# The first token tile in two halves on two DMA queues, the second tile behind it on ScalarE's queue

## Chip, cores and metric

The kernel runs on one core of one Trainium2 chip. The metric is the device time of one execution in microseconds (us); lower is better. All times here come from the profile, from the trace behind it, or from timed runs of the kernel.

## What is computed

A transformer block with attention and a gated feed-forward layer side by side, over 2048 tokens of width 576, in bfloat16:

```python
xn  = layernorm(x)                       # eps 1e-5, no weights
qkv = xn @ wqkv                          # 32 heads of 18, q, k and v
p   = softmax(mask(q @ k.T * 18**-0.5))  # causal, window of 256 tokens
A   = (p @ v) @ wo
B   = (silu(xn @ w1) * (xn @ w3)) @ w2   # inner width 4608
out = x + A + B
```

## The kernel before

The tokens go in four chunks of 512, each of four tiles of 128 tokens (one token per partition). For each chunk the kernel normalises the four tiles, transposes them so that the width lies on partitions (`xnT`, and `xnS`, the same with the halves of the partitions swapped), projects q, k and v, runs the 36 units of the feed-forward layer's first stage (line L712) with the score, exponent and value steps of attention spread among them, and then the second stage with `w2` and `wo` (L778). The normalisation and transposes of chunks 1 to 3 are done during the chunk before; only those of chunk 0 stand in front of everything. Most matmuls work on 64 rows, two at a time on the two halves of the array.

The program is written as a list of operations. `add` appends one to its engine ("sp", "act", "pe", "dve", "pool": SyncE, ScalarE, TensorE, VectorE, GpSimd) together with the buffers it reads (`r`), writes first (`w`) or writes jointly with others (`j`). From these the waits are worked out; each engine runs its operations strictly in the order of the list. DMAs are issued on SyncE's or ScalarE's queue, and each buffer `xp0` to `xp6` has a semaphore of its own for its DMAs: a reader waits for the count that all its writers add up to. A DMA that an engine issues is one of its instructions, and what stands behind it on that engine comes after the issue.

The start of chunk 0, in the order of the list as far as the change touches it:

- GpSimd makes the identity (L280, L281) for the transposes and the constant -0.5 for the power.
- `load_x` (L292) fetches tiles 0 to 3 of `x`, 128 rows of 1152 bytes each: tile 0 on SyncE's queue, tiles 1, 2 and 3 on ScalarE's. SyncE goes on with the value weights `wv` (L821, L825), the query and key weights (L847, L851, into the buffer `pt`) and later the feed-forward weights (L316).
- VectorE clears `oq` (L827) and the query buffer `qv` (L828). TensorE runs nine matmuls on the zeros of `oq` (`warm`, L832) whose results nobody reads, then two more that wait for tile 0's variance.
- Tile 0's statistics are taken on VectorE (`ln_stats`: two halves with L376, their sum with L379, plus epsilon in L356). Tile 1's are taken on ScalarE (`ln_stats_act`): one pass for the mean (L366), one for the variance (L368), each with an accumulator read, and a small GpSimd operation (L370) that turns the first sum into the mean. Tiles 2 and 3 are done on VectorE.
- `ln_root` raises variance plus epsilon to the power -0.5 on GpSimd (L358).
- `ln_apply` writes the normalised tile `xn` (L399 on VectorE: 512 columns, then the last 64 twice). For tile 1 the last 64 columns go another way: GpSimd computes a shift (L391) and ScalarE applies it (L394).
- `xn_turn` transposes a tile with ten small matmuls (L414); the last pair takes the last 64 columns. ScalarE copies the result to `xnT` in two parts (L427); for tile 3 VectorE copies one of them.
- `warm_halves` (L838) is two more matmuls on zeros. `proj_begin` and `proj_end` run the two parts of a projection (L476); the four tiles' value projections alternate with the transposes, and q and k follow.

The order in the list around the change is written out by hand: tile 0's statistics, the two waiting matmuls, tile 1's statistics on ScalarE, the power of tile 0, the application of tile 0, the power of tile 1, the transposes of tile 0, the first part of its value projection, then VectorE's first half of tile 2's statistics, the application of tile 1, and so on. Nothing but this order and the waits sets when an instruction runs.

Of the kernel before, what the change touches and what calls it, by code (L numbers as in the profile page):

```python
# [44 lines left out]
class _Prog:  # L45
# [13 lines left out]
    def add(self, eng, fn, r=(), w=(), j=(), dma=None, after=()):  # L59
        deps = []  # L60
        for k in r:
            deps += self.bufs[k].writers
        for k in w:
            g = self.bufs.get(k)
            if g is not None:
                deps += g.ahead(eng)
        for k in j:
            g = self.bufs[k].before
            if g is not None:
                deps += g.ahead(eng)  # L70
        op = _Op(eng, fn, deps + list(after), dma)
        op.after = tuple(after)
        self.n[eng] += 1
        op.pos = self.n[eng]
        if dma is not None:
            self.dma_count[dma] = self.dma_count.get(dma, 0) + 16
            op.cnt = self.dma_count[dma]
        for k in r:
            self.bufs[k].readers.append(op)
        for k in w:  # L80
            self.bufs[k] = _Gen([op], self.bufs.get(k))
        for k in j:
            self.bufs[k].writers.append(op)
        for k in w:
            if self.bufs[k].before is not None:
                self.bufs[k].before.before = None
        self.ops.append(op)
        return op
# [76 lines left out]
def bass_parallel_sum__sliding_block__glu_gated_swiglu__prompt_kernel(  # L165
# [27 lines left out]
    x2 = A_x[0]  # L193
    out2 = out[0]
    P = _Prog(nc)
    add = P.add

    with ExitStack() as es:

        def sb(name, shape, dtype=dt.bfloat16):  # L200
            return es.enter_context(nc.sbuf_tensor(name, shape, dtype))
# [4 lines left out]
        xp = [sb(f"xp{i}", [128, D]) for i in range(NXP)]  # L206
# [78 lines left out]

        xp_ctr = 0

        def load_x(t, eng="sp"):
            nonlocal xp_ctr
            s = xp_ctr % NXP  # L290
            xp_ctr += 1
            add(eng, lambda e: e.dma_start(xp[s][:], x2[t * 128:(t + 1) * 128, :]), w=[("xp", s)], dma=f"xp{s}")  # L292
            return s

        nfill = 0
# [57 lines left out]
        def ln_root(t, eng=None):  # L353
            i = t % 2
            if eng is not None:
                return add(eng, lambda e: e.tensor_scalar(vpe[i][:], mv[i][:, 1:2], 1e-5, None, op0=ALU.add),  # L356
                           r=[("mv", i)], w=[("vpe", i)])
            return add("pool", lambda e: e.tensor_tensor(rstd[i][:], vpe[i][:], neghalf[:], ALU.pow),  # L358
                       r=[("vpe", i), "neghalf"], w=[("rstd", i)])

        def ln_stats_act(t, s):
            i = t % 2
            junk = hT[:, 0:3, :].rearrange("p t c -> p (t c)").bitcast(dt.float32)[:, 0:D]
            keys = [("h", n) for n in range(3)]
            root = float(D) ** 0.5
            add("act", lambda e: e.activation(junk, xp[s][:], ACT.Copy, scale=-1.0 / (D * root), accum_out=vpe[i][:]),  # L366
                r=[("xp", s)], w=[("vpe", i), *keys])
            add("act", lambda e: e.activation(junk, xp[s][:], ACT.Square, bias=vpe[i][:], scale=1.0 / root, accum_out=mv[i][:, 1:2]),  # L368
                r=[("xp", s), ("vpe", i)], w=[("mv", i), *keys])
            add("pool", lambda e: e.tensor_scalar(mv[i][:, 0:1], vpe[i][:], -root, None, op0=ALU.mult),  # L370
                r=[("vpe", i)], j=[("mv", i)])

        def ln_stats(t, s, part):
            i = t % 2
            if part < 2:
                add("dve", lambda e: e.bn_stats(stats[i][:, part, :], xp[s][:, part * HD:part * HD + HD]),  # L376
                    r=[("xp", s)], **{"j" if part else "w": [("stats", i)]})
                return
            add("dve", lambda e: e.bn_aggr(mv[i][:], stats[i][:]), r=[("stats", i)], w=[("mv", i)])  # L379
            if t >= TB:  # L380
                ln_root(t, "pool")
                ln_root(t)

        def ln_apply(t, s, parts=(0, 1)):

            i = t % 2
            for n in parts:
                both = xn[i][:, 512:640].rearrange("p (a c) -> p a c", a=2)
                end = xp[s][:, 512:D].unsqueeze(1).to_broadcast([128, 2, 64])
                if n == 2:  # L390
                    add("pool", lambda e: e.tensor_scalar(  # L391
                        shift[i][:], mv[i][:, 0:1], rstd[i][:, 0:1], -1.0, op0=ALU.mult, op1=ALU.mult),
                        r=[("mv", i), ("rstd", i)], w=[("shift", i)])
                    add("act", lambda e, dst=both, src=end: e.activation(  # L394
                        dst, src, ACT.Identity, bias=shift[i][:], scale=rstd[i][:, 0:1]),
                        r=[("xp", s), ("shift", i), ("rstd", i)], w=[("xnd", i)])
                    continue
                dst, src = (both, end) if n else (xn[i][:, 0:512], xp[s][:, 0:512])
                add("dve", lambda e, dst=dst, src=src: e.tensor_scalar(  # L399
                    dst, src, mv[i][:, 0:1], rstd[i][:, 0:1], op0=ALU.subtract, op1=ALU.mult),  # L400
                    r=[("xp", s), ("mv", i), ("rstd", i)], w=[("xnd" if n else "xn", i)])
# [415 lines left out]

        xslot = {}
        for t in range(TB):
            xslot[t] = load_x(t, "act" if t else "sp")  # L820
        add("sp", lambda e: e.dma_start(  # L821
            wv[:, 0:4, :], A_wqkv[0:512, 2 * D:3 * D].rearrange("(kd p) f -> p kd f", p=128)),
            w=["wv"], dma="wv")
# [6 lines left out]
        def warm(b, n, after=()):  # L830
            for k in range(n):
                add("pe", lambda e: e.matmul(PS[:, b, :], oq[:, 0:128], oq[:], start=True, stop=True),  # L832
                    r=["oq0"], after=after, **{"j" if k else "w": [("ps", b)]})
# [10 lines left out]
        for h in range(2):  # L844
            for n in range(2):
# [3 lines left out]
                    dma=f"wqk{h}", **{"j" if n else "w": [f"wqk{h}"]})  # L849
# [34 lines left out]
        for p in range(3):  # L884
            ln_stats(0, xslot[0], p)
        warm(4, 2, (ln_root(0, "dve"),))
        ln_stats_act(1, xslot[1])
        ln_root(0)
        ln_apply(0, xslot[0])
        ln_root(1, "pool")  # L890
        ln_root(1)
# [67 lines left out]
        for c in range(NC):  # L959
# [70 lines left out]
            for u in range(NF):  # L1030
# [3 lines left out]
                if u in loads:  # L1034
                    for i in loads[u]:
                        xslot[(c + 1) * TB + i] = load_x((c + 1) * TB + i)
# [12 lines left out]
                if next_pv in pv_ready and clock >= pv_ready[next_pv] and next_pv < 3:  # L1049
                    j = next_pv  # L1050
# [20 lines left out]
                if u in stat:  # L1071
                    t = (c + 1) * TB + stat[u]
# [4 lines left out]
                if u in apply:  # L1077
                    t = (c + 1) * TB + apply[u]
# [5 lines left out]
                if c == 0 and u == 13:  # L1084
                    for t in range(4):
# [3 lines left out]
                            dma="wo", **{"j" if t else "w": ["wo"]})  # L1089
                if c == 0 and u == 18:  # L1090
                    rows = A_wo[0:4 * Dh, :].rearrange("(n d) f -> n d f", d=Dh)
                    add("sp", lambda e: e.dma_start(wo[126:128, 0:4, :], rows[:, 0:2, :].rearrange("n d f -> d n f")),
                        j=["wo"], dma="wo")
                    for p in range(2):
                        add("sp", lambda e, p=p: e.dma_start(wo[64 * p:64 * p + 64, 4, :], rows[:, 2:Dh, :]),
                            j=["wo"], dma="wo")
                if c == 0 and u in (20, 22, 24, 26):
                    load_w2(0, (u - 20) // 2, "act" if u < 24 else "sp")
                if u == 31:
                    xs = [load_x(c * TB + tt) for tt in range(TB)]  # L1100
# [9 lines left out]
            n = -3  # L1110
            for item in p2_list(c):
# [25 lines left out]
                elif n in (100, 120) and c + 2 < NC:  # L1137
                    t = (c + 2) * TB + (n == 120)
# [34 lines left out]
```

## Time and profile before

| What | Value |
|---|---|
| Median of 3 runs | 558.82 us (558.53 to 558.98) |
| The profiled execution's own time | 558.68 us |
| Its span in the profile | 556.9 us |
| TensorE busy | 552.9 us, 99% of the span |
| VectorE, ScalarE, GpSimd busy | 310.2, 255.1, 163.5 us |
| DMA | 86.07 MB, mean 155 GB/s |
| First matmul of the projections (L476) | starts at 6.96 us |
| First matmul of the feed-forward stage (L712) | starts at 21.41 us |

Busy time is the time in which an engine has an instruction of its own under way. Matmuls are pipelined, so a busy TensorE also holds the time in which one waits for its turn in the array; how far it is from its best is read from the distance between starts. In the timeline a row is a group of like instructions: its start, its time, engine, line, operation, tiles written and read, shape and count, and in brackets the idle time before it and what ended it. "SPq" and "ACTq" are the issues of DMAs on the two queues; the time of an issue is that of the issuing engine and not of the transfer. "PEld" are weight loads of TensorE.

### The profile page before, as it was taken

Reading aid. Unit: us, or ns where it says so; the run is one execution under the profiler, and the core shown is the slowest. Engines: PE = TensorE matmul, PEld = TensorE weight load, DVE = VectorE, ACT = ScalarE, POOL = GpSimd, SP = SyncE. Lnnn points to the kernel's source line nnn. Section 1 sums busy time; section 2 is a strip of 40 time slices with the busy share of each in tenths; the row PEclk is TensorE's granted clock in tenths of the full one; section 3 lists DMA queues with packets and bytes.
Section 4 is the critical chain, followed back from the end, with each engine's and each line's share of the span. In section 5 each row is a group of like instructions: output and inputs, shape, how many; then the busy total and the mean of one; then the engine's idle time right before and its main releaser. Section 6 shows DMA issues by size and latency. Waiting matters only on the chain.

```text
span 556.9 us, 18212 instructions
## 1 busy us (share of the span) xinstructions
PE 552.9 (99%) x8013; PEld 351.1 (63%) x8013; DVE 310.2 (56%) x584; ACT 255.1 (46%) x357; POOL 163.5 (29%) x384
## 2 busy tenths in 40 slices
PE   8999999999999999999999999999999999999998
PEld 4566445677687455477777645547777654555776
DVE  7566788710466778851056668884105567767211
ACT  5357776100287776600047776650005667676000
POOL 6413454400033445330003344533000333433000
PEclk9999999999999999999999999999999999999999
DMA  9997999578566656656846746467683674551650
GB/s 247 210 189 167 206 206 217 144 180 190 137 136 144 145 137 160 156 147 178 201 109 140 171 110 170 124 162 160 171 195 86 137 171 124 151 135 31 164 151 22
DMA packets 127893, 86.07 MB, mean 155 GB/s; under 512 B 35430, under 2 KB 125502, under 8 KB 127814
## 3 DMA queue, kind: packets, MB, share of 16 engines
q1 hardware_dynamic: 88994, 62.88, 48.8%
q10 hardware_dynamic: 38820, 22.02, 16.1%
q8 instruction: 63, 1.03, 0.8%
q14 instruction: 16, 0.13, 0.1%
HBM read 71.37 MB, written 2.36 MB: 132 GB/s over the span
## 4 chain that ended last, share of the span: by engine, by line
PE 99%; DVE 0%; ACT 0%; issue 0%
PE ps L712 51%; PE ps L778 29%; PE ps L476 10%; PE ps L596 6%; PE ps L653 4%; PE ps L832 1%; PE ps L414 0%; DVE ofin L797 0%; ACT xnT L427 0%; DVE oq L827 0%
## 5 line engine op out<-in xcount | busy, mean ns | idle before, releaser
L712 PE MATMUL ps<-xnT,w 64*128 64x512 bf16 x1400 | 182.7, 376 | 0.0
L712 PE MATMUL ps<-xnS,w 64*128 64x512 bf16 x1120 | 155.6, 376 | 0.0
L778 PE MATMUL ps<-w,hT 64*128 64x288 bf16 x2288 | 143.7, 283 | 0.0
L727 DVE SCALAR_TENSOR_TENSOR gs<-th,ps 128x512 bf16<-128x512 bf16 x144 | 98.0, 681 | 80.2 <-ACT th L721 78.8
L605 ACT ACTIVATE pt<-ps 128x1024 bf16<-128x1024 f32 (+1 forms) x112 | 113.3, 1011 | 63.7 <-PE ps L596 62.7
L778 PEld LDWEIGHTS ps<-w,hT 64*128 64x128 bf16 x2288 | 111.9, 94 | 29.4 <-issue 0.2
L712 PEld LDWEIGHTS ps<-xnT,w 64*128 64x128 bf16 x1400 | 75.0, 94 | 53.9
L632 POOL TENSOR_TENSOR pt<-pt,mk 128x128 int32<-128x128 int32 (+1 forms) x199 | 80.6, 427 | 79.3 <-ACT pt L605 79.3
L730 DVE SCALAR_TENSOR_TENSOR hT<-gs,ps 128x512 bf16<-128x512 bf16 x144 | 98.9, 687 | 4.9
L721 ACT ACTIVATE th<-ps 128x512 bf16<-128x512 f32 x144 | 85.5, 593 | 23.5 <-PE ps L712 23.2
L712 PEld LDWEIGHTS ps<-xnS,w 64*128 64x128 bf16 x1120 | 61.0, 94 | 49.3
L797 DVE TENSOR_TENSOR ofin<-ps,xp 128x288 bf16<-128x288 f32 x32 | 12.7, 452 | 125.7 <-PE ps L778 125.7
L489 ACT ACTIVATE stage<-ps 128x512 bf16<-128x512 f32 x16 | 9.6, 598 | 143.6 <-PE ps L476 143.6
L632 POOL TENSOR_TENSOR hT<-hT,mk 128x128 int32<-128x128 int32 (+1 forms) x31 | 12.4, 422 | 169.7 <-ACT hT L605 169.7
L596 PE MATMUL ps<-qv,kv 64*128 64x320 bf16 (+4 forms) x528 | 54.0, 260 | 0.0
L596 PEld LDWEIGHTS ps<-qv,kv 64*128 64x128 bf16 x528 | 28.9, 94 | 24.1 <-ACT pt L605 0.3
L476 PE MATMUL ps<-xnT,wp 64*128 64x512 bf16 (+1 forms) x360 | 39.1, 355 | 0.0
L605 ACT ACTIVATE stage<-ps 128x1024 bf16<-128x1024 f32 x24 | 24.6, 1025 | 12.5 <-PE ps L596 12.5
L675 DVE STREAM_TRANSPOSE od<-oq 128x256 bf16<-128x256 bf16 x64 | 25.8, 427 | 6.3 <-POOL oq L668 6.3
L476 PEld LDWEIGHTS ps<-xnT,wp 64*128 64x128 bf16 x360 | 20.4, 94 | 12.8
L476 PE MATMUL ps<-wv,xnT 64*128 64x288 bf16 x288 | 22.4, 284 | 0.2 <-ACT xnT L427 0.2
L632 POOL TENSOR_TENSOR stage<-stage,mk 128x128 int32<-128x128 int32 (+1 forms) x42 | 17.0, 423 | 17.3 <-ACT stage L605 17.2
(68 smaller groups left out, 337.4 us busy)
## 6 DMA issues: line engine op xcount, KB each, us to landing
w<-in_B_w_dram SPq DMA_DIRECT2D x210, 192.0 KB, 4.1
w<-in_B_w_dram ACTq DMA_DIRECT2D x70, 288.0 KB, 3.5
xp<-in_A_x_dram SPq DMA_DIRECT2D x29, 144.0 KB, 3.5
out_dram<-ofin SPq DMA_DIRECT2D x32, 72.0 KB, 3.0
xnS<-xnT SPq DMA_DIRECT2D x8, 256.0 KB, 5.2
oT<-od SPq DMA_DIRECT2D x56, 36.0 KB
pt<-in_A_wqkv_dram SPq DMA_DIRECT2D x4, 288.0 KB, 5.8
hT<-in_B_w_dram SPq DMA_DIRECT2D x6, 192.0 KB, 7.7
```

Source lines behind the costliest of these rows:

```text
L476: op = add("pe", lambda e, out_=out_, st=st, mv=mv, n=n, r0=r0, first=first: e.matmul(out_, st, mv, start=first, stop=(part == 1 and n == ...
L596: add("pe", lambda e, r0=r0, out_=out_, kb=kb, q0=q0, nb=nb: e.matmul(out_, kb4[r0:r0 + 64, g, kb + NV - NB, :] if kb < 0 else kv[r0:r0 + ...
L605: add("act", lambda e: e.activation(pt_slot(sl)[:, 0:w, :], PS[:, SC[0]:SC[1] + 1, 0:w].rearrange("p r q -> p q r"), ACT.Exp, scale=scale) ...
L632: add("pool", lambda e, vb=vb, mm=mm: e.tensor_tensor(vb, vb, mm, ALU.mult), r=(key if n == 0 else []) + ["mk"], **{"w" if n == 0 else "j" ...
L653: add("pe", lambda e, p=p, q=q, pr=pr, sl=sl, g=g, pos=pos, q0=q0, nb=nb, col=col, first=first, n=n: e.matmul(PS[32 * q:32 * q + VW, banks ...
L675: add("dve", lambda e: e.transpose(od[i][:, g % 2, c0:c0 + CH // 2], oq[:, c0:c0 + CH // 2]), r=["oq", "oq0"], **{"j" if half or g % 2 els ...
L712: op = add("pe", lambda e, n=n, r0=r0, r=r, k=k, src=src: e.matmul(PS[:, b0 + r, :], wt[r0:r0 + 64, k, fl * 128:(fl + 1) * 128], src, star ...
L721: add("act", lambda e: e.activation(th[i][:], PS[:, bg, :], ACT.Tanh, scale=0.5), r=[("ps", bg)], w=[("th", i)])
L727: add("dve", lambda e: e.scalar_tensor_tensor(out=gs[i][:], in0=th[i][:], scalar=1.0, in1=PS[:, bg, :], op0=ALU.add, op1=ALU.mult), r=[("t ...
L730: add("dve", lambda e: e.scalar_tensor_tensor(out=hT[:, u, :], in0=gs[i][:], scalar=0.5, in1=PS[:, bu, :], op0=ALU.mult, op1=ALU.mult), r= ...
L778: op = add("pe", lambda e: e.matmul(PS[:, bank, 0:HD], stat, move, start=new, stop=False, skip_group_check=True, **tile), r=keys, after=he ...
L797: add("dve", lambda e: e.tensor_tensor(ofin[:, o, :], PS[:, bank, 0:HD], xp[xs[n]][:, d0:d0 + HD], ALU.add), r=[("ps", bank), ("xp", xs[n] ...
```

## The change

Tile 0 is fetched by two DMAs of 64 rows: rows 0 to 63 on ScalarE's queue and rows 64 to 127 on SyncE's. Tiles 1, 2 and 3 stay on ScalarE's queue, now behind the first half of tile 0, so that ScalarE issues four DMAs in place of three. Readers of tile 0 wait until both halves have landed. In addition the power of tile 0 on GpSimd (`ln_root(0)`) is put ahead of tile 1's statistics, of which one operation (L370) runs on GpSimd. Every other load has one piece, as before.

```diff
-        def load_x(t, eng="sp"):
+        def load_x(t, eng="sp", pieces=1):
             nonlocal xp_ctr
             s = xp_ctr % NXP
             xp_ctr += 1
-            add(eng, lambda e: e.dma_start(xp[s][:], x2[t * 128:(t + 1) * 128, :]), w=[("xp", s)], dma=f"xp{s}")
+            for n in range(pieces):
+                a, b = 128 * n // pieces, 128 * (n + 1) // pieces
+                add(eng if n == 0 else "sp", lambda e, a=a, b=b: e.dma_start(xp[s][a:b, :], x2[t * 128 + a:t * 128 + b, :]),
+                    dma=f"xp{s}", **{"j" if n else "w": [("xp", s)]})
             return s
...
         for t in range(TB):
-            xslot[t] = load_x(t, "act" if t else "sp")
+            xslot[t] = load_x(t, "act", 2 if t == 0 else 1)
...
         for p in range(3):
             ln_stats(0, xslot[0], p)
         warm(4, 2, (ln_root(0, "dve"),))
+        ln_root(0)
         ln_stats_act(1, xslot[1])
-        ln_root(0)
         ln_apply(0, xslot[0])
```

## The prediction

> **What bounds the kernel now.** I read the page first: engine shares, then the chain that ended last.
>
> ```profile
> PE 552.9 (99%) x8013; PEld 351.1 (63%) x8013; DVE 310.2 (56%) x584; ACT 255.1 (46%) x357; POOL 163.5 (29%) x384
> ...
> PE 99%; DVE 0%; ACT 0%; issue 0%
> ```
>
> TensorE is busy 552.9 of 556.9 us and carries 99% of the chain. Start to start, the L712 matmuls keep 0.216 us a pair almost everywhere, so nothing behind the start can be won. The edit touches only the first microseconds, so I read the timeline from 0 to 8 us (columns: start, length, engine, line, operation, tiles):
>
> ```profile
> 0.80 0.40 SPq L292 DMA_DIRECT2D xp<-in_A_x_dram  x1
> 0.80 1.45 ACTq L292 DMA_DIRECT2D xp<-in_A_x_dram  x3
> ...
> 1.24 4.87 PE L832 MATMUL ps<-oq 128*128 128x512 bf16 x11 [1.24 <-DVE oq L827]
> ...
> 1.56 1.76 DVE L828 MEMSET qv<- 128x2048 f32 x1 [0.38 <-issue]
> ...
> 2.28 1.28 ACT L366 ACT_TABLE_LOAD   x1 [2.28 <-issue]
> ...
> 3.66 0.82 DVE L376 BATCH_NORM_STATS2 stats<-xp 128x6 f32<-128x288 bf16 x2 [0.34 <-DMA xp<-in_A_x_dram]
> ...
> 3.84 0.68 ACT L366 ACTIVATE hT<-xp 128x576 f32<-128x576 bf16 x1 [0.28 <-DMA xp<-in_A_x_dram]
> ...
> 4.70 0.24 POOL L370 TENSOR_SCALAR mv<-vpe 128x1 f32<-128x1 f32 x1 [0.90 <-ACT hT L366]
> ...
> 5.03 0.57 POOL L358 TENSOR_TENSOR rstd<-vpe,neghalf 128x1 f32<-128x1 f32 x1
> ...
> 5.63 0.64 DVE L399 TENSOR_SCALAR xn<-xp,mv,rstd 128x512 bf16<-128x512 bf16 x2 [0.72 <-POOL rstd L358]
> 5.92 0.57 POOL L358 TENSOR_TENSOR rstd<-vpe,neghalf 128x1 f32<-128x1 f32 x1
> 6.10 0.33 PEld L414 LDWEIGHTS ps<-ident,xn 64*128 64x128 bf16 x10 [0.89 <-DVE xn L399]
> ...
> 6.55 0.40 DVE L399 TENSOR_SCALAR xn<-xp,mv,rstd 128x512 bf16<-128x512 bf16 x1
> 6.60 0.40 POOL L391 TENSOR_SCALAR shift<-mv,rstd 128x1 f32<-128x1 f32 x1
> ...
> 7.08 0.49 ACT L394 ACTIVATE xn<-xp,shift,rstd 128x128 bf16<-128x128 bf16 x1
> ```
>
> Tile 0's statistics are on VectorE (3.66), tile 1's on ScalarE (3.84). Both waits ended with the tile's DMA. Tile 0's normalised rows reach TensorE at 6.10, tile 1's at 7.68 (7.79 for the last pair of transposes, which needs L394). The busy time of L832 is filler: real work begins at 6.10. From 5.91, where the filler's columns end, to 11.54 TensorE has short gaps of 0.19, 0.37, 0.11, 0.06, 0.12 and 0.12 us, in sum 0.97; after that it is full to the end. Last, the windows view of the first transfers (last column GB/s):
>
> ```profile
> 1.80:2.20 0.40, 0.40 (x3) 0.13 (x1) 0.40 (x1) 0.00 (x0) 0.34 (x2) 1.00 1.08 138
> ...
> 2.60:3.00 0.40, 0.40 (x3) 0.12 (x2) 0.40 (x1) 0.40 (x1) 0.40 (x2) 1.00 1.07 360
> ```
>
> The DMA engines are taken from 1.8 us on, slowly at first: transfers compete, and what goes ahead delays what is behind.
>
> **The change, part by part.** The sum goes against the profiled execution: 558.68 us, of which 556.9 span and 1.78 around it; the median of the runs is 558.82, 0.14 above.
>
> *Tile 0 in halves.* Tiles 0 to 3 land at 3.64, 3.82, 5.06 and 6.45. In the DMA packets of the trace, tile 0's 128 rows run from 1.83 to 2.97 on SP's queue and tile 1's from 1.99 to 3.30 on ScalarE's; half of them are over at 2.58 and 2.82. With 64 rows on each queue tile 0 is over at about 2.8 instead of 2.97, and with the same 0.52 to 0.67 to the landing it lands at 3.35 to 3.5. VectorE's memset (L828) ends at 3.33, so the statistics start at 3.4, 0.26 earlier. The rest is as now: vpe at 4.65, POOL's power 4.72 to 5.29, L399 at 5.33, first transposes possible at 5.74. But the eleven filler matmuls stand ahead of them in TensorE's order until 5.91: the gain is 0.19, not 0.26. The Trainium skill, "DMA: Bandwidth & Descriptors", Rules for kernel authors, speaks against halves: they share the same 16 engines, so one 128-partition transfer is to be used. By it the term is 0; the sum below is the same, since tile 1 decides it.
>
> *Tile 1 behind a half on ScalarE's queue.* Its issue moves from 0.80 to 1.24 (one issue is 0.42 to 0.52). Lower bound: only this shift, landing at 3.82 + 0.44 = 4.26. Upper bound: it takes the whole place of today's tile 2, 5.06. Between them, by packets: 64 + 128 rows are over on this queue where half of tile 2 is over today, at 4.02, plus 0.44 to 0.52 to the landing: 4.5, which I take, because the queue behind the first half is then beside wv on SP's queue just as tile 2 is now. That is 0.7 later.
>
> *A fourth issue on ScalarE.* Queued behind it there: the table load, then everything else of ScalarE. The load moves from 2.28 to 2.8 and ends at 4.1 instead of 3.56. Tile 1's data at 4.5 cover this; with earlier data it would hold the first ACTIVATE at 4.1, 0.27 late, all the same.
>
> *POOL's order.* Tile 0's power now stands ahead of tile 1's L370, which would run at about 5.4 with tile 1 so late and hold tile 0's power from 4.72 to 5.6. The swap avoids this 0.9; against today it brings nothing more than the 0.04 between 4.99 and 5.03.
>
> *What is late next.* Tile 1: ScalarE starts at 4.52, is through both passes 1.68 later at 6.20, POOL starts 0.09 later and needs 0.89 for vpe and power: 7.18 (now 6.49). L399 of tile 1 starts at 7.24 instead of 6.55, 0.69 late. POOL L391 ends at 7.68, L394 at 8.26, and TensorE's last pair of tile 1's transposes goes from 7.79 to 8.30: 0.51 late, with everything of TensorE behind it. VectorE is in order too: tile 2's statistics (half), its apply, tile 3's apply are all queued behind L399 of tile 1. Their ends go from 9.06 to 9.75 and from 10.67 to 11.36, and TensorE's last pairs of tiles 2 and 3 from 9.26 to 9.80 and from 10.81 to 11.40. So 0.59 arrives where TensorE becomes full, and 0.19 of tile 0 is lost before it.
>
> *At nothing.* SP issues as many DMAs as before, the first smaller; wv lands no later. Tile 2 (about 5.9) and tile 3 (at most 7.1) are used at 6.19 and 7.67; should they be later by 0.5 the wait for tile 1 still hides it. The wait on two landings holds what waited for one. Later tiles use one transfer as before.
>
> Sum: +0.6 us, 559.28 against the profile, **559.4** against the median.
>
> **Rivals.** Differences under 0.2% (1.1 us) are about what a measurement of this kernel can tell from no change.
>
> *Tile 1 in tile 2's place, 5.06.* ScalarE's second pass then ends at 6.75 and also holds tile 0's eviction, 6.43 today; L399 of tile 1 is 1.24 late and TensorE about 1.15: 560.0. For: ScalarE's queue moved hardly anything between 3.2 and 3.6 when tile 2 stood behind tile 1 beside wv. Against: today's first half of tile 2 was over by 4.02.
>
> *TensorE's rate rises later: slower.* The fillers are 0.43 apart for 512 columns, later 0.216; the first L476 pairs of 288 columns are 0.19, 0.16, then 0.12 apart, so the rate doubles near 7.2 (the windows' clock column, 1.00 from the start, has no record before that). The change opens a gap of about 0.5 at 7.8. If the rise falls behind it and is put off until tile 3's projection (10.6), the 21 pairs between, 0.12 each, take 2.5 more, of which the new gaps hide about 1: +1.5 on top of part of the 0.6, 560.4 to 560.9. It decides from the point where the rise moves beyond 8.3. Against: until 7.2 the change leaves TensorE busier, not idler. The Trainium skill, "TensorE: Matmul & The Clock Gate", Part 1, has the clock rise after a busy window of some 3.4 us that runs free of the kernel; the rise at 7.2 after a start at 1.24 fits, and no run here shows another phase.
>
> *Tile 0 leads.* Tile 1's delay is covered and 0.2 of tile 0 stays: 558.6. Against: the table load alone holds tile 1 to 4.1.
>
> *Faster by over 0.2%.* It needs 1.1 us, and all gaps of TensorE after 5.91 sum to 0.97. Only something the trace doesn't show would do it: 557.5.
>
> **How the numbers follow.** Forecast, +0.2 to +0.9: 0.48. Tile 2's place: 0.14. Late rate: 0.20. Tile 0 leads: 0.10. Faster: 0.08. The middle rival counts as slower, so slower 0.34, same 0.48 + 0.10 = 0.58, faster 0.08. The forecast's own range is 559.0 to 559.7. The range 558.4 to 560.7 leaves out the fast case and about half of the late rate, 0.18.
>
> **What would show it.** After: VectorE's first statistics at 3.35 to 3.5; TABLE_LOAD at 2.8; ScalarE's first ACTIVATE near 4.5; POOL L358 of tile 0 ahead of L370; first transposes at 5.9; tile 1's L399 near 7.2; a TensorE gap of half a us before the last transposes of tile 1; L712 starting near 22.0 instead of 21.4. It is wrong if tile 1's first ACTIVATE stands at 4.2 or earlier, if VectorE catches up by tile 3, or if L476 pairs stay 0.24 apart beyond 8.3.

## The result

The changed kernel takes 562.60 us (median of six runs, 561.95 to 563.89) against 558.66 us of the kernel before (six runs, 558.50 to 558.98): 0.72% slower, ratio 1.0072 with a 95% interval of 1.0059 to 1.0085. The prediction said 559.4 us and no measurable difference; it was wrong, and its range (up to 560.7) did not hold the result. The profiled execution is the fastest of the six: 561.95 us, with a span of 560.1 us instead of 556.9.

First the page of the changed kernel: engine shares and the chain that ended last, by engine and by line. The lines behind L292 have moved by 3 (L712 is L715 here).

```profile
PE 553.7 (99%) x8013; PEld 345.9 (62%) x8013; DVE 310.6 (55%) x584; ACT 255.0 (46%) x357; POOL 163.6 (29%) x384
...
PE 98%; DMA 1%; ACT 0%; ACTq 0%; DVE 0%; issue 0%
PE ps L715 50%; PE ps L781 28%; PE ps L479 10%; PE ps L599 6%; PE ps L656 3%; DMA xp<-in_A_x_dram 1%; ACT hT L371 0%; ACT hT L369 0%; PE ps L417 0%; ACTq L294 0%; DVE ofin L800 0%; ACT xnT L430 0%
```

TensorE's share of the chain falls from 99% to 98%, and a DMA of `x` now stands in it with 1%. Before, no DMA did. In order of time (start, length, what) the chain of the kernel before starts with the fillers:

```profile
1.24 4.87 PE ps L832 x11
6.12 0.29 PE ps L414 x4
...
6.43 0.39 ACT xnT L427
...
6.96 0.89 PE ps L476 x10
```

That of the changed kernel says which DMA it is:

```profile
0.80 0.62 ACTq L294
...
1.46 5.10 DMA xp<-in_A_x_dram
...
6.57 0.78 ACT hT L369 x2
...
7.38 0.87 ACT hT L371 x2
8.25 0.28 ACT xnT L430
...
8.66 1.38 PE ps L479 x10
```

It holds the issue of tile 0's first half (0.80), then tile 1's transfer from its issue at 1.46 to its landing at 6.55, then tile 1's two passes on ScalarE, and only then the eviction of tile 0's transposes (ScalarE's copy of them to `xnT`), which stands behind those passes in ScalarE's order. Of the fillers at the start, nothing is left in the chain. The timeline, with the rows that answer to those of before:

```profile
0.79 0.61 SPq L294 DMA_DIRECT2D xp<-in_A_x_dram  x1
0.80 2.51 ACTq L294 DMA_DIRECT2D xp<-in_A_x_dram  x4
...
1.46 0.56 SPq L824 DMA_DIRECT2D wv<-in_A_wqkv_dram  x1
...
3.35 1.28 ACT L369 ACT_TABLE_LOAD   x1 [3.35 <-issue]
...
3.68 0.82 DVE L379 BATCH_NORM_STATS2 stats<-xp 128x6 f32<-128x288 bf16 x2 [0.35 <-DMA xp<-in_A_x_dram]
...
5.02 0.55 POOL L361 TENSOR_TENSOR rstd<-vpe,neghalf 128x1 f32<-128x1 f32 x1 [1.21 <-DVE vpe L359]
...
6.57 0.68 ACT L369 ACTIVATE hT<-xp 128x576 f32<-128x576 bf16 x1 [1.95 <-DMA xp<-in_A_x_dram]
...
8.63 0.57 POOL L361 TENSOR_TENSOR rstd<-vpe,neghalf 128x1 f32<-128x1 f32 x1
8.66 1.38 PE L479 MATMUL ps<-wv,xnT 64*128 64x288 bf16 x10 [2.05 <-ACT xnT L430]
...
9.24 0.41 DVE L402 TENSOR_SCALAR xn<-xp,mv,rstd 128x512 bf16<-128x512 bf16 x1 [1.14 <-POOL rstd L361]
```

Tile 0's statistics start at 3.68 (before 3.66): the halves won nothing. Tile 1's first pass starts at 6.57 instead of 3.84, its application on VectorE (L402, before L399) at 9.24 instead of 6.55, both 2.7 late. TensorE has a gap of 2.05 before the value projection, and the first feed-forward matmul starts at 24.43 instead of 21.41. From there to the end both kernels need nearly the same (535.7 and 535.5), so 3.0 of the 3.2 by which the spans differ arise before the feed-forward stage. The windows view adds a second effect (the last three columns are TensorE's granted clock, the DMA share and GB/s):

```profile
2.60:3.40 0.80, 0.80 (x4) 0.25 (x3) 0.73 (x1) 0.05 (x1) 0.80 (x2) 1.00 0.71 135
...
8.40:11.80 3.40, 3.11 (x34) 1.96 (x36) 2.49 (x9) 1.82 (x5) 1.67 (x4) 0.50 1.13 259
```

From 8.42 to 11.83 the granted clock is 0.50. In the kernel before it rises once, at 7.21, and stays. And between 2.6 and 3.4 the DMA engines move 135 GB/s where the kernel before moved 324:

```profile
2.60:3.40 0.80, 0.80 (x4) 0.25 (x3) 0.72 (x1) 0.80 (x1) 0.80 (x2) 1.00 1.06 324
```

### The profile page after: what moved, and what is told of

The parts are those of the page before. It is cut to its first block, busy times and chain, and to the rows that moved or that the text cites. A ratio compares the mean times of both kernels' runs of the same rounds, so it can differ in the third digit from the quotient of the medians.

```text
span 560.1 us, 18213 instructions
## 1 busy us (share of the span) xinstructions
PE 553.7 (99%) x8013; PEld 345.9 (62%) x8013; DVE 310.6 (55%) x584; ACT 255.0 (46%) x357; POOL 163.6 (29%) x384
## 4 chain that ended last, share of the span: by engine, by line
PE 98%; DMA 1%; ACT 0%; ACTq 0%; DVE 0%; issue 0%
PE ps L715 50%; PE ps L781 28%; PE ps L479 10%; PE ps L599 6%; PE ps L656 3%; DMA xp<-in_A_x_dram 1%; ACT hT L371 0%; ACT hT L369 0%; PE ps L417 0%; ACTq L294 0%; DVE ofin L800 0%; ACT xnT L430 0%
## 5 line engine op out<-in xcount | busy, mean ns | idle before, releaser
L715 PE MATMUL ps<-xnT,w 64*128 64x512 bf16 x1400 | 182.0, 376 | 0.0
L715 PE MATMUL ps<-xnS,w 64*128 64x512 bf16 x1120 | 155.0, 376 | 0.0
L715 PEld LDWEIGHTS ps<-xnT,w 64*128 64x128 bf16 x1400 | 72.8, 94 | 56.0
L715 PEld LDWEIGHTS ps<-xnS,w 64*128 64x128 bf16 x1120 | 59.3, 94 | 50.9
L479 PE MATMUL ps<-xnT,wp 64*128 64x512 bf16 (+1 forms) x360 | 39.0, 355 | 0.0
L479 PEld LDWEIGHTS ps<-xnT,wp 64*128 64x128 bf16 x360 | 20.1, 94 | 13.0
L479 PE MATMUL ps<-wv,xnT 64*128 64x288 bf16 x288 | 23.4, 295 | 2.0 <-ACT xnT L430 2.0
```

The lines of the kernel that those rows point to most:

```text
L479: op = add("pe", lambda e, out_=out_, st=st, mv=mv, n=n, r0=r0, first=first: e.matmul(out_, st, mv, start=first, stop=(part == 1 and n == ...
L715: op = add("pe", lambda e, n=n, r0=r0, r=r, k=k, src=src: e.matmul(PS[:, b0 + r, :], wt[r0:r0 + 64, k, fl * 128:(fl + 1) * 128], src, star ...
```

## The experiments

The experiments part four theories. Theory A: tile 1 is late because it is handed over (its issue ends) after `wv`'s transfer of 512 rows and then stands behind it. Theory B: ScalarE's queue itself is late behind a half. Theory C: the two queues only share bandwidth. Theory D: the loss is tile 1's lateness and, on top, TensorE's second stretch at half rate.

The table sums up every run, from its profile (us) and its timed runs. "Handed over" is the end of tile 1's issue minus that of `wv`'s 512 rows (in e7, of the first quarter); "first row" is the start of tile 1's first packet, counted in order on its queue; "projection" is the first value matmul, "FF" the first feed-forward matmul. Behind a median below stand its ratio to the kernel before, measured beside it, and the 95% interval of the ratio.

| Kernel | Handed over | First row | Tile 1 lands | wv lands | Projection | FF | Median |
|---|---|---|---|---|---|---|---|
| before | -0.46 | 1.99 | 3.82 | 5.85 | 6.96 | 21.41 | 558.66 |
| after | +0.28 | 4.47 | 6.55 | 6.89 | 8.66 | 24.43 | 562.60 |
| e1 tile 1 on SP | -0.48 | 2.66 | 3.87 | 7.84 | 7.88 | 22.34 | 559.74 |
| e2 wv last | -1.00 | 3.09 | 4.46 | 9.40 | 9.45 | 25.03 | 562.86 |
| e3 halves on one queue | -1.47 | 1.82 | 3.19 | 7.23 | 7.85 | 23.67 | 561.01 |
| e4 tile 1 second | +0.03 | 3.17 | 5.39 | 5.63 | 8.48 | 23.12 | 561.64 |
| e5 order alone | -0.46 | 1.99 | 3.56 | 5.87 | 6.61 | 21.81 | 559.20 |
| e6 filler | +0.28 | 3.88 | 6.82 | 7.26 | 8.93 | 24.52 | 561.94 |
| e7 wv in quarters | +0.28 | 3.09 | 4.93 | 8.28 | 8.33 | 24.03 | 561.13 |
| e8 column halves | +0.02 | 2.74 | 5.13 | 7.02 | 7.24 | 22.83 | 560.57 |
| e9 eviction first | +0.28 | 3.94 | 6.71 | 6.80 | 6.85 | 25.94 | 563.06 |
| e10 tile 1 third | +0.58 | 4.85 | 6.33 | 5.61 | 9.43 | 25.01 | 562.78 |
| e11 small one ahead | +0.37 | 3.87 | 7.15 | 6.67 | 10.23 | 25.86 | 563.33 |
| e12 order undone | +0.28 | 3.72 | 6.76 | 6.98 | 9.90 | 26.28 | 563.42 |
| e13 mean on VectorE | -0.46 | 1.99 | 3.76 | 5.74 | 6.79 | 21.48 | 558.69 |
| e14 tile 1 third, new order | +0.57 | 5.02 | 6.66 | 6.22 | 8.77 | 25.39 | 562.80 |

**e1: tile 1 ahead of wv on SP's queue.**

```diff
-            xslot[t] = load_x(t, "act", 2 if t == 0 else 1)
+            xslot[t] = load_x(t, "sp" if t == 1 else "act", 2 if t == 0 else 1)
```

> The changed kernel, with tile 1 on SP's queue between the second half of tile 0 and wv; tiles 2 and 3 stay on ScalarE's queue behind the first half. Theory A (transfers of both queues are served in the order of their issue, so tile 1 waited for wv's 512 rows): tile 1's first row goes out near 2.8 instead of 4.47 and it lands at 3.8 to 4.4 instead of 6.55; 558.8 to 559.6 us, and tile 2, now behind wv, is the next to be late. Theory B (what stands behind a first half on ScalarE's queue starts late, whatever SP issues): tile 1 is early as well, tile 2 lands near 6.5 and the time is the same; this run alone does not part them. Theory C (it is only bandwidth shared with wv): tile 1 lands near 4.5 at best and the time stays over 560.

559.74 us (1.0022; 1.0010 to 1.0034). Tile 1 lands at 3.87, and 2.9 of the 3.9 us are gone. Against theory C: tile 1's bytes share the engines as before. Against theory B: tile 2, now right behind the half on ScalarE's queue and handed over 0.20 ahead of `wv`, lands at 4.70 and not near 6.5; tile 3, handed over 0.28 behind `wv`, lands at 7.64. What is late now is `wv`, as it stands behind: 7.84, and the projection starts at 7.88. The runs fall in two groups: six with a granted clock of 1.000 take 559.02 to 559.90, four with 0.997 take 560.71 to 561.21. So a second stretch at half rate costs about 1.5 here, where little else hides it.

**e2: wv's 512 rows behind its two small pieces.** The statement with `wv[:, 0:4, :]` is moved below the loop with `wv[64 * p:64 * p + 64, 4, :]`.

> The changed kernel, with wv's 512 rows issued behind its two small pieces of 64 rows instead of ahead of them; ScalarE's queue is as in the changed kernel. Theory A: tile 1 now waits for 64 rows only and its first row goes out near 3.0; it lands at 4.0 to 4.7, 559.0 to 560.0 us, with wv later (near 7.2) but not later than its use by more than 0.5. Theory B: tile 1 still starts at 4.3 to 4.6, lands at 6.3 to 6.7, 562 to 563 us.

Tile 1's first row goes out at 3.09 and it lands at 4.46: theory A, not B, for tile 1. But the time is 562.86 (1.0073; 1.0058 to 1.0088), because `wv` lands at 9.40, 2.2 later than expected, and becomes the wait itself (projection at 9.45). The late `wv` was mis-sized by me.

**e3: tile 0 in two halves, both on SP's queue, all else as before.**

```diff
-            xslot[t] = load_x(t, "act" if t else "sp")
+            xslot[t] = load_x(t, "act" if t else "sp", 1 if t else 2)
```

(with both pieces on `eng`)

> The kernel before, with tile 0 alone in two halves, both on SP's queue ahead of wv; ScalarE's queue and GpSimd's order as before. It shows what the halves do by themselves. If halves bring tile 0 forward: landing at 3.3 to 3.5, first statistics 0.2 earlier, 558.4 to 558.7 us. If a transfer of 64 rows starts later than one of 128 (2.17 and 2.47 instead of 1.83 and 1.99 in the changed kernel): landing at 3.7 to 4.1, tile 1 unchanged near 3.8, 558.7 to 559.3 us. In no case the 4 us of the change, by theory A and B alike.

561.01 us (1.0042; 1.0027 to 1.0057), more than any case expected. The two issues of 64 rows take 0.61 and 0.57 on SP in place of one of 0.40; tile 0's second half lands at 4.61 and `wv`, issued 0.8 later than before, at 7.23. TensorE also falls back to half rate, from 8.19 to 11.60 in the profile; three of the four runs have a mean clock of 0.997. Two halves on one queue cost by themselves.

**e4: tile 2 ahead of tile 1, whole tiles.** `for t in (0, 2, 1, 3)` in the loop of the loads of the kernel before.

> The kernel before, with tile 2 issued ahead of tile 1 on ScalarE's queue and nothing else: tile 1 takes the place that tile 2 had, landing at 5.06. It gives the price of tile 1's lateness by itself. If the sum of the prediction is right in its chain (each us of tile 1's lateness beyond 0.2 arrives at TensorE), 559.7 to 560.1 us and L712 starts 1.0 to 1.2 later. If lateness costs more than itself because the clock falls in the gap, 560.5 or more and a granted clock under 1.

Tile 1 lands at 5.39 and the feed-forward stage starts 1.7 later; 561.64 us (1.0052; 1.0035 to 1.0070), over the expected 560.1. Here GpSimd has the old order, so tile 0's power waits for tile 1's first pass (6.60 instead of 5.03) and TensorE waits 1.6 for tile 0's transposes: a cost that the sum left out. That accounts for the profiled run, 560.40. The five runs go up to 563.02, and only one of them has a mean clock under 1. The clock column has no record before a run's first rise, so a rise that came late, as in the prediction's rival, would not show in it; no trace of the longer runs is kept, and their time stays open.

**e5: GpSimd's new order alone, on the kernel before.**

```diff
+        ln_root(0)
         ln_stats_act(1, xslot[1])
-        ln_root(0)
```

> The kernel before, with GpSimd's power of tile 0 put ahead of tile 1's statistics and nothing else. All theories: nothing, 558.5 to 558.8 us, since tile 1's operation on GpSimd ends 0.08 before the power starts today. If it differs by more than 0.5 us, the order has a cost that was not seen.

559.20 us (1.0010; 1.0001 to 1.0020): 0.56 lost, where I expected nothing. GpSimd's timeline of this run:

```profile
4.75 0.55 POOL L358 TENSOR_TENSOR rstd<-vpe,neghalf 128x1 f32<-128x1 f32 x1 [0.94 <-DVE vpe L356]
5.38 0.40 POOL L370 TENSOR_SCALAR mv<-vpe 128x1 f32<-128x1 f32 x1
5.95 0.22 POOL L356 TENSOR_SCALAR vpe<-mv 128x1 f32<-128x1 f32 x1 [0.16 <-POOL mv L370]
6.25 0.57 POOL L358 TENSOR_TENSOR rstd<-vpe,neghalf 128x1 f32<-128x1 f32 x1
```

Tile 1's mean (L370) used to run in GpSimd's idle time, at 4.70. Now it stands between the two powers, and tile 1's power starts at 6.25 instead of 5.92, though tile 1 landed 0.26 earlier than in the profile of before.

**e6: fillers in TensorE's gap.** `warm(0, 9)` behind `warm_halves(JOBS[0])` in the changed kernel.

> The changed kernel, with nine more matmuls on zeros (full array, 512 columns) behind the two of tile 0's transposes, so that TensorE's gap of 2.05 us is filled; they end before the value projection could start. Theory D (the loss is tile 1's lateness and, on top, a second stretch at half rate that the gap brings): the granted clock stays 1.0 behind its first rise, and the time falls by 1.0 to 1.7 to 560.9 to 561.6 us. If lateness alone is the cause: 562.2 to 562.8. If the rate alone is the cause: 558.6 to 559.2.

561.94 us (1.0058; 1.0040 to 1.0076), between the two theories' ranges. The granted clock stays at 1.0 in all four runs, so the second stretch at half rate is the doing of TensorE's idle time. By the medians it is worth 0.66 (562.60 - 561.94); the intervals of the two ratios overlap, so this size is rough. Windows of this run:

```profile
8.40:11.80 3.40, 2.37 (x38) 1.27 (x38) 2.40 (x9) 2.02 (x7) 1.74 (x4) 1.00 1.14 247
```

TensorE is busy 2.37 of the 3.40 at full rate where it was busy 3.11 at half rate: it waits for tile 1 instead. By the medians, lateness is about 3.3 of the loss and the rate about 0.7.

**e7: wv in four transfers of 128 rows.**

```diff
-        add("sp", lambda e: e.dma_start(wv[:, 0:4, :], ...), w=["wv"], dma="wv")
+        for q in range(4):
+            add("sp", lambda e, q=q: e.dma_start(wv[:, q, :], A_wqkv[128 * q:128 * q + 128, 2 * D:3 * D]),
+                dma="wv", **{"j" if q else "w": ["wv"]})
```

> The changed kernel, with wv's first 512 rows in four transfers of 128 rows on SP's queue instead of one of 512. Theory A (tile 1 stands behind a whole transfer of 512 rows, because it is handed over 0.3 later than that): it now stands behind one or two of 128, its first row goes out at 3.0 to 3.6 and it lands at 4.2 to 5.2; 559.3 to 560.6 us. Theory B (ScalarE's queue itself is late behind a half): first row at 4.3 or later, landing over 6, 562 us or more. Theory C (shared bandwidth alone): the same bytes on the other queue, so no change either, 562 us or more.

Tile 1's issue is as in the changed kernel (1.47 to 2.30), the same bytes go on SP's queue, and its first row goes out at 3.09 instead of 4.47; it lands at 4.93, as theory A has it and neither B nor C. So what counts is not the moment at which tile 1's issue ends, but what is handed over ahead of it. The time is 561.13 (1.0043; 1.0029 to 1.0057), over the expected range, since the last quarter of `wv` now lands at 8.28 behind tiles 2 and 3:

```profile
8.33 1.07 PE L479 MATMUL ps<-wv,xnT 64*128 64x288 bf16 x10 [1.97 <-DMA wv<-in_A_wqkv_dram]
```

**e8: tile 0 halved by columns.**

```diff
-                a, b = 128 * n // pieces, 128 * (n + 1) // pieces
+                a, b = D * n // pieces, D * (n + 1) // pieces
...  xp[s][:, a:b], x2[t * 128:(t + 1) * 128, a:b]
```

> The changed kernel, with tile 0 halved by columns (128 rows of 576 bytes each) instead of by rows. If it is the 64 rows that make the issue long (0.61 instead of 0.40, and 0.84 for the one behind it): issues of 0.40 to 0.45, tile 1 handed over at 1.7 and landing at 4.3 to 5.2, 559.3 to 560.8 us. If it is having two transfers at all, or the small size: issues of 0.6, tile 1 landing over 6, 562 us or more.

```profile
0.79 0.40 SPq L294 DMA_DIRECT2D xp<-in_A_x_dram  x1
0.80 1.93 ACTq L294 DMA_DIRECT2D xp<-in_A_x_dram  x4
...
5.15 0.69 ACT L369 ACTIVATE hT<-xp 128x576 f32<-128x576 bf16 x1 [1.11 <-DMA xp<-in_A_x_dram]
```

With 128 rows the issues take 0.40 and 0.41, ScalarE's four take 1.93 instead of 2.51, tile 1 is handed over 0.02 behind `wv` instead of 0.28, and lands at 5.13; 560.57 us (1.0037; 1.0026 to 1.0047). The 64 rows made the issues long.

**e9: the eviction ahead of tile 1's statistics on ScalarE.** In the changed kernel `ln_stats_act(1, xslot[1])` is moved behind `xn_turn(0, ...)`.

> The changed kernel, with ScalarE's eviction of tile 0's transposes put ahead of tile 1's statistics in ScalarE's order (in the changed kernel it stood behind them until 8.15). If the eviction that is held is what sets the time: the value projection starts near wv's landing at 7.0 instead of 8.66, TensorE's gap falls to 0.7, and 560.5 to 561.5 us. If tile 1's own chain sets the time (statistics, power, VectorE's queue): little is won, 562.0 to 563.2 us, since tile 1's statistics start no earlier.

The projection starts at 6.85, 1.8 earlier, and the time is 563.06 (1.0077; 1.0062 to 1.0092), no better. (The stretch at half rate is longer in its profile, 6.83; but its one run with a mean clock of 0.997 takes 562.46, and those of the change with that clock 561.95 to 562.64.) The eviction that ends TensorE's gap in the chain is not the cause; tile 1's own chain is.

**e10 and e14: whole tiles in the order 0, 2, 3, 1,** first with GpSimd's old order, then with the new one. `for t in (0, 2, 3, 1)` in the loop of the loads, and in e14 the swap of e5.

> The kernel before, with whole tiles in the order 0 on SP and 2, 3, 1 on ScalarE's queue: tile 1 lands at 6.3 to 6.7, about where the change put it, with wv and tile 0 in time. If tile 1's landing is the whole cause of the change's loss: 561.6 to 562.8 us, like the change. If late wv, late tiles 2 and 3 or tile 0 in halves hold a share of their own: less than 561.5 us.

> The kernel before with whole tiles in the order 0 on SP and 2, 3, 1 on ScalarE's queue, as run once, now with GpSimd's new order, so that it differs from the changed kernel only in tile 0 being whole, wv in time (5.6) and tiles 2 and 3 ahead of tile 1. Tile 1 lands at 6.3 to 6.6. If its landing alone carries the change's loss: 562.0 to 562.8 us. If the late wv or the late tiles 2 and 3 hold a share: 560.8 to 561.8 us.

562.78 (1.0077; 1.0062 to 1.0093) and 562.80 us (1.0069; 1.0049 to 1.0088). In e14 tile 0 is whole, tiles 2 and 3 are early, `wv` lands 0.7 earlier than in the changed kernel, tile 1 lands at 6.66, and the loss is that of the change. A late tile 1, with the idle time of TensorE that it brings, is enough for it.

**e11: 64 rows that nobody needs ahead of tile 1 on ScalarE's queue,** in the kernel before, with tile 0 whole on SP:

```diff
+        add("act", lambda e: e.dma_start(xp[6][0:64, :], x2[0:64, :]), w=[("xp", 6)], dma="xp6")
         for t in range(TB):
```

> The kernel before, with a transfer of 64 rows that nobody needs (rows of x into a buffer that is still free) ahead of tile 1 on ScalarE's queue; tile 0 stays whole on SP's queue and GpSimd's order is that of before. Theory A (a 64-row issue of 0.61 and 0.84 for the one behind it, so tile 1 is handed over 0.3 or more behind wv and stands behind its 512 rows): tile 1 lands at 6.0 to 7.0 and 561.3 to 562.8 us. If the two halves on two queues are needed for it: tile 1 lands at 4.5 to 5.3, 559.3 to 560.5 us.

```profile
0.79 0.40 SPq L292 DMA_DIRECT2D xp<-in_A_x_dram  x1
0.80 0.60 ACTq L819 DMA_DIRECT2D xp<-in_A_x_dram  x1
1.44 1.59 ACTq L292 DMA_DIRECT2D xp<-in_A_x_dram  x3
...
7.17 0.68 ACT L366 ACTIVATE hT<-xp 128x576 f32<-128x576 bf16 x1 [2.83 <-DMA xp<-in_A_x_dram]
```

One small transfer of 0.60 ahead of tile 1 is enough: it is handed over 0.37 behind `wv`, lands at 7.15, and the kernel takes 563.33 us (1.0081; 1.0064 to 1.0098), over the expected 562.8. The old order adds to it, since tile 0's power now waits to 8.36.

**e12: GpSimd's old order in the changed kernel.**

> The changed kernel, with GpSimd's old order (tile 1's operation L370 of before ahead of tile 0's power). The prediction said that the new order avoids a loss: tile 0's power now waits for tile 1's first pass, to 7.7 instead of 5.0, tile 0's transposes come near 8.9, and the time is 562.8 to 564.5 us. If tile 1's chain hides it all: 562.2 to 562.8 us. If the new order only costs: below 562.2.

563.42 us (1.0086; 1.0071 to 1.0101), by the medians 0.8 slower than the change. Tile 0's power goes to 7.97 and its transposes to 9.05, so the wait that the prediction named is there. What it costs is less sure: the two intervals overlap, and e10 and e14, which differ in this order alone, take the same time (562.78 and 562.80).

**e13: the new order with tile 1's mean (L370) on VectorE,** in the kernel before: the swap of e5, and `add("dve", ...)` for that operation.

> The kernel before with GpSimd's new order, and with tile 1's small mean operation (L370) on VectorE, where it falls into the idle time between tile 0's variance and its application. If the 0.57 us of the new order alone are this operation standing between the two powers: tile 1's power starts 0.3 to 0.5 earlier than with the order alone, 558.2 to 558.7 us, at least as good as before. If the order costs for another reason: 559.0 to 559.4 us as with the order alone.

558.69 us, the kernel before on the same chip 558.68 (0.9997; 0.9988 to 1.0006). Tile 1's power starts at 5.85. The loss of e5 was the operation's place on GpSimd.

## Why the prediction was wrong

**The step that failed: "Tile 1 behind a half on ScalarE's queue".** I put its landing between 4.26 and 5.06 and took 4.5; it was 6.55. Both the size of the issue and the bound were wrong.

- The issue: I priced it at "0.42 to 0.52", by the 128-row issues of ScalarE. The nearest rows were those of 64 rows: L825 on SP's queue, 0.58 to 0.59 each. The half takes 0.62, and the issue behind it 0.82 to 0.84 in every run with a row half on ScalarE ahead of it. So tile 1 is handed over at 2.29 and not near 1.7, and `wv` at 2.02 passes it.
- The bound: I took "the whole place of today's tile 2, 5.06" for the worst case. But tile 2 was handed over 0.02 behind `wv`. The row that stood 0.57 behind it was tile 3: first row at 4.96, landing at 6.45. The table shows the rule of this kernel: handed over ahead of `wv` or at most 0.03 behind it, tile 1's first row goes out at 1.8 to 3.2; 0.28 or more behind, at 3.7 to 5.0; with `wv` in quarters, at 3.1 again. In the seven traces with 0.28 or more and `wv` whole, tile 1's first row goes out when 88 to 475 of `wv`'s 512 rows have gone, and its last only when 510 to 512 have. The bound stood in the trace, in tile 3's row.

**Right in the main: the chain from tile 1 to TensorE.** I had each us of lateness arrive at TensorE less about 0.1. In the two profiles with the new order, a late tile 1 and no second stretch at half rate, tile 1 at 5.13 (e8) and 6.82 (e6) put the feed-forward stage at 22.83 and 24.52: 1.42 for 1.31 and 3.11 for 3.00, so each arrives whole and 0.1 more. With the true landing the sum would have given about 561.4 before the rate. The place of the wait was another: I saw it before the last transposes of tile 1, and it stood before tile 0's value projection, since tile 0's eviction waits behind tile 1's passes on ScalarE. Only my rival with tile 1 at 5.06 had that eviction held.

**The rival of the rate: right in kind, wrong in place and price.** I saw a gap of 0.5 that might put off the rise. The gap was 2.05, and it did not put off the rise but undid it: all six runs of the change have a mean clock of 0.993 to 0.997. The sign that I named, pairs of L476 still 0.24 apart beyond 8.3, did come (L479 here, until 11.8). The price was about 0.7 and not 1.5, since TensorE would have waited for tile 1 anyway. In the other rival, "hardly anything" was too strong: between 3.2 and 3.6 ScalarE's queue started 19 rows in the kernel before, SyncE's 85.

**Tile 0 in halves: nothing, where I had 0.19.** Over the profiles, tile 0 in row halves on two queues lands at 3.66, 3.37, 3.32, 3.37, 3.40, 3.32 and 3.46 (after, e1, e2, e6, e7, e9, e12), whole at 3.64, 3.38, 3.38, 3.45, 3.39 and 3.12 (before, e4, e5, e10, e14, e11). The rows of a half start later (2.17 and 2.47 instead of 1.83 and 1.99), which takes back what fewer rows give. The rule of the Trainium skill, "DMA: Bandwidth & Descriptors", Rules for kernel authors, which has halves of the partitions not worth while, agrees with these numbers.

**GpSimd's order: half right.** The wait that it avoids inside the change is there (tile 0's power at 7.97 in e12, at 5.02 in the change); I priced it at 0.9, and the medians differ by 0.8, which e10 and e14 don't confirm. By itself it costs 0.56 (e5) where I had a gain of 0.04: I did not list L370 in its new place as a cost, because I followed tile 0's power alone and not what was moved in front of tile 1's.

**At nothing: `wv` "no later".** It lands at 6.89 instead of 5.85; in e1, e2 and e7, where tile 1 was helped, it became the next wait. Tiles 2 and 3 land at 7.62 and 8.33, where I had 5.9 and at most 7.1; the wait for tile 1 hid them, as I had argued, for in e14 they are early and the loss is the same.

## What to carry to other kernels

In this kernel the first transfers are a queue of their own: count for each not its bytes but when its issue ends, and which large transfer of the other queue is handed over before it. To price a transfer that is moved behind another, look in the trace for one that already stands in that relation to the large transfer, not for the one whose place it takes. And what is moved ahead on an in-order engine moves everything else behind it: price both.

## What the runs showed of the hardware

The first issue of a queue takes 0.60 to 0.63 with 64 rows and 0.40 to 0.42 with 128, and the issue behind a row half on ScalarE takes 0.82 to 0.84 (0.60 in e11, where SP's tile was whole).

The two queues don't simply share. In the runs in which tile 1 is handed over ahead of `wv`, its first row follows the end of its issue by 0.63 to 0.79. In the changed kernel, handed over at 2.29, it was thus due at about 3.0 and came at 4.47. Between 3.0 and 3.4 the DMA engines had room (the kernel before first, then the changed one):

```profile
3.00:3.40 0.40, 0.40 (x3) 0.12 (x2) 0.33 (x1) 0.40 (x1) 0.40 (x1) 1.00 1.05 288
```

```profile
3.00:3.40 0.40, 0.40 (x3) 0.12 (x2) 0.33 (x1) 0.05 (x1) 0.40 (x1) 1.00 0.29 49
```

They were taken for 0.29 of the time, and tile 1 still waited. The halves alone don't bring this dip: e1, with the same two, moves 282 GB/s between 2.6 and 3.4, where the change moves 135. What brings it, and what holds the later transfer, stays open.

TensorE's first rise comes at any time from 3.97 to 7.21 in these profiles, after the same first matmul at 1.24, and a second stretch at half rate lasts 3.41 or 6.83. The Trainium skill, "TensorE: Matmul & The Clock Gate", Part 1, has a window of 3413 ns that runs free of the kernel, and the lengths of the stretches and the spread of the rises, 3.24, fit. But the first rise can come 2.73 after the first matmul (e6), and the clock can fall without a gap as long as the window: 2.05 was enough in the change, and two gaps of 0.86 and 0.50 in e3. In these 16 profiles it goes by the busy time of TensorE in the 3.41 us behind the first rise: with 0.52 to 1.79 us of it the clock fell at their end (nine profiles, e3 the busiest), with 1.85 or more it stayed (seven, e1 the least busy). The margin is small and the ends of matmuls are modelled, so this is a count of the profiles and not a threshold.
